# Memory attention and an erf-softplus FFN: blocks of 384 tokens across batches, and the second product with g stationary

## The chip, the cores and the metric

The kernel runs on one core of a Trainium2 chip. The metric is the device time of one execution in microseconds (us). Engines are named as in the profile: PE multiplies matrices (PEld is its loading of the stationary operand), ACT applies functions to tiles, DVE does arithmetic on tiles, POOL is hardly used, SP issues the DMAs in order.

## What is computed

Eight batches of 576 tokens, 8 heads of 64 dimensions, 32 memory slots a head. The attention gathers k and v into the slots with a softmax over the tokens, and reads them with a softmax over the slots; the FFN (512 to 2048 to 512) follows on all 4608 tokens.

```python
a = softmax(phi, axis=tokens)                  # (b, h, s, m)
k_m = einsum('bhsm,bhsd->bhmd', a, k); v_m = einsum('bhsm,bhsd->bhmd', a, v)
attn = softmax(q @ k_m.T / 8, axis=slots)
x = (attn @ v_m), heads side by side           # (4608, 512)
h = x @ w_in
g = h * erf(softplus(h))
out = g @ w_out                                # (4608, 512)
```

The weights come as 64-bit floats; the kernel reads them as pairs of 32-bit words.

## The kernel before

**Operands.** Products that must be exact enough are made from two parts: `split` (L114 to L116) puts a rounded copy in `hi` (ACT, type fp32r) and the rest in `lo` (DVE), and `products` (L374) takes hi x hi, hi x lo and lo x hi. So each product below is three matmuls. `erf(softplus(h))` is a product of a tanh and three factors (`FACTORS`, L29): `ffn1` makes the tanh (L397, ACT) and the first product (L398, DVE), `factor` the three others (L411 or L413 on ACT, L414 on DVE), `g_split` the two parts of g (L422 ACT, L423 DVE).

**Folding.** `vw` (L317) multiplies v_m of a batch with w_in once, so that the first FFN product runs over the 256 slots (8 heads x 32) of the attention weights instead of over 512 dimensions. `heads` (L302) does it for 8 heads, four at a time in one of two row halves; the scores (L335) use it too. One `vw_pair` makes 512 of the 2048 hidden columns; a batch has four pairs. The pool `vwp` holds four pairs.

**Steps.** The unit `u` is half a batch, U = 288 tokens, so there are 16 units, and each is taken in NPR = 8 chunks of 256 hidden columns: NS = 128 steps. Step `i` issues `ffn1(i, 0)`, a factor of step i-1, `ffn1(i, 1)`, two more factors, `g_split(i-2)`, and merged with these `ffn2(i-3, d)` for the four blocks d of 128 output columns. `ffn1` is 12 matmuls of 128x128 stationary (vw) by 128x288 moving (attention weights). `ffn2` is 24 matmuls with w_out stationary and g (128x288) moving; it adds up in four PSUM tiles over the eight chunks of a unit, which are then copied out (L453) and stored transposed (L454, `outT`).

**Side work.** The attention of a later unit or batch lies in lists by step (`batch_tasks` L456, `unit_tasks` L467) and is merged into the steps before it is needed: `phi_max`, `phi_exp` (the softmax over tokens), `kmvm`, `block_diag` (k_m and v_m in the layout of `heads`), `vw_pair`, and for each unit `scores`, `sm_max`, `sm_norm`, `sm_back`. In the first eight steps the weights are decoded too: `decode_1` (DVE L142, ACT L145 and L146), `decode_2` (DVE L159 and L162), `decode_3` (w_out only: ACT L174, PE L177 and L178, ACT L179). The weights come in 20 pieces, 12 of 1 MB and 8 of 512 KB; LEAD = 7 of them are decoded ahead of step 0.

**Order.** The list `prog` is the order in which the work is written. The tile framework then orders each engine's queue with a time model of its own, taking ready work forward; for DVE a window (`WINDOW`) limits by how much. SP's queue is in the order that results. Loads are written as soon as a buffer of their kind has room (`fill`, `frees`, `loads`); `FIRST` is the order of the first ones.

**Memory.** Tiles come from pools with a fixed number of buffers; a tile that takes a buffer waits for the last reader of the tile that had it. `f` (three buffers) holds a factor; `ost` (two buffers) holds outputs until they are stored; `gp` (three buffers) holds g.

Of the kernel before, what the change touches and what calls it, by code (L numbers as in the profile page):

```python
# [25 lines left out]


# [9 lines left out]
def tile_memory_attention_then_erf_softplus_ffn(  # L37
# [3 lines left out]
    k: bass.AP,  # L41
    v: bass.AP,
# [4 lines left out]
    outT: bass.AP,  # L47
# [4 lines left out]
    H = k.shape[2]  # L52
# [3 lines left out]
    DM = outT.shape[0]  # L56
    NDM = DM // P
    NP_ = H // 2
    NG = 2
    U = S // 2  # L60
    NB = U // 32
    NPR = DFF // 256
    NU = 2 * B
    NS = NU * NPR
    NF = len(FACTORS)
    SC = [(c * P, min(P, S - c * P)) for c in range((S + P - 1) // P)]
    RAW_BUFS = 3
    STAGED = 6
    FIRST = "wo phiT start phi wo raw raw wo raw start wo q".split()
    LEAD = 7  # L70
    WINDOW = {mybir.EngineType.DVE: (12, 28)}
    PO = 5
    SO = 2
    VL = 4
    VB = 1
# [4 lines left out]
    vwp = ctx.enter_context(tc.tile_pool(name="vwp", bufs=NPR // 2))  # L80
# [4 lines left out]
    gp = ctx.enter_context(tc.tile_pool(name="gp", bufs=3))  # L85
    raw_pool = ctx.enter_context(tc.tile_pool(name="raw", bufs=RAW_BUFS))
    ost = ctx.enter_context(tc.tile_pool(name="ost", bufs=2))
    ps_h = ctx.enter_context(tc.tile_pool(name="ps_h", bufs=2, space=PSUM))
    ps_o = ctx.enter_context(tc.tile_pool(name="ps_o", bufs=1, space=PSUM))
    ps_a = ctx.enter_context(tc.tile_pool(name="ps_a", bufs=2, space=PSUM))  # L90
# [8 lines left out]
    def column(value, name):  # L99
        t = const.tile([P, 1], F32, name=name)  # L100
        nc.vector.memset(t, value)
        return t

    tb = column(GB, "tb")
    fb = [column(f[1] if f[0] == "Q" else f[2], f"fb{i}") for i, f in enumerate(FACTORS)]
# [14 lines left out]
    def load_weight(*key):  # L120
        name, c, r, n = key
        if n == NP_:
            t = wop.tile([P, NP_ * 256], I64, name="w_" + name, tag="wo")
        else:
            t = raw_pool.tile([P, n * 256], I64, name="raw")
        if name == "in":
            nc.sync.dma_start(
                out=t.rearrange("p (r f) -> p r f", r=n),
                in_=w_in[:, r : r + n, c * 256 : (c + 1) * 256],
            )  # L130
        else:
            nc.sync.dma_start(
                out=t.rearrange("p (r d) -> p r d", d=DM),
                in_=w_out[:, 2 * c + r : 2 * c + r + n // 2],
            )
        st[key] = t

    def decode_1(*key):
        v = st[key].bitcast(I32).rearrange("p (n two) -> p n two", two=2)
        lo, hi = v[:, :, 0], v[:, :, 1]  # L140
        hf = hi.bitcast(F32)
        nc.vector.tensor_scalar(  # L142
            out=hf, in0=hf, scalar1=TOP, scalar2=-TOP, op0=ALU.min, op1=ALU.max
        )
        nc.scalar.activation(lo, lo.bitcast(U32), AF.Identity, scale=LOW)  # L145
        nc.scalar.activation(hf, hf, AF.Identity, scale=REBIAS)  # L146

    def decode_2(*key):
        name, c, r, n = key
        v = st[key].bitcast(I32).rearrange("p (n two) -> p n two", two=2)  # L150
        lo, hi = v[:, :, 0], v[:, :, 1]
        dst = hi
        if name == "in":
            if r == 0:
                if c % 2 == 0:
                    w_in_sb[c // 2] = const.tile([P, NP_, 512], F32, name=f"w_in{c // 2}")
            dst = w_in_sb[c // 2].bitcast(I32)[:, r : r + n, c % 2 * 256 : (c % 2 + 1) * 256]
            hi, lo = (x.rearrange("p (r f) -> p r f", f=256) for x in (hi, lo))
        nc.vector.scalar_tensor_tensor(  # L159
# [4 lines left out]
        )  # L164

    def decode_3(*key):
        name, c, r, n = key
        t = st.pop(key)
        if name == "out":
            w = t.bitcast(F32).rearrange("p (r d two) -> p r d two", d=DM, two=2)[:, :, :, 1]  # L170
            if r == 0:
                wo[c] = wop.tile([P, 2, 2, DM], F32R, name="wo", tag="wo")
            hi, lo = (wo[c][:, x, r : r + n // 2] for x in range(2))
            nc.scalar.activation(hi, w, AF.Identity)  # L174
            for x in range(n // 2):
                ps = ps_a.tile([P, DM], F32, name="psa")
                nc.tensor.matmul(out=ps, lhsT=ident, rhs=w[:, x], start=True, stop=False)  # L177
                nc.tensor.matmul(out=ps, lhsT=minus, rhs=hi[:, x], start=False, stop=True)  # L178
                nc.scalar.activation(lo[:, x], ps, AF.Identity)  # L179

    def load_phiT(b, g):
        if (b, g) == (0, 1):
            t = wop.tile([P, S], F32, name="phiT", tag="wo")
        else:
            t = att.tile([P, S], F32, name="phiT")
# [3 lines left out]
    def load_phi(b):  # L189
        t = att.tile([P, len(SC), H * M], F32, name="phi")  # L190
        n = S // P
        s0, ln = SC[-1]
        nc.sync.dma_start(
            out=t[:, :n], in_=phi[b, : n * P].rearrange("(c p) e -> p c e", p=P)
        )
        if ln < P:
            nc.sync.dma_start(out=t[:ln, n], in_=phi[b, s0 : s0 + ln])
        st["a", b] = t

    def load_kv(b, p):  # L200
        if b == 0 and p == NP_ - 1:
            t = wop.tile([P, len(SC), 2, 2, D], F32, name="kv", tag="wo")
        else:
            t = raw_pool.tile([P, len(SC), 2, 2, D], F32, name="raw")
        n = S // P
        s0, ln = SC[-1]
        h = 2 * p
        for x, src in enumerate((k, v)):
            src = src[b, :, h : h + 2]
            nc.sync.dma_start(  # L210
                out=t[:, :n, x], in_=src[: n * P].rearrange("(c p) h e -> p c h e", p=P)
            )
            if ln < P:
                nc.sync.dma_start(out=t[:ln, n, x], in_=src[s0 : s0 + ln])
        for j in range(2):
            st["kv", b, h + j] = t[:, :, :, j, :]

    def load_q(u):
        b, hf = divmod(u, 2)
        t = att.tile([P, NP_, U], F32, name="q")  # L220
        nc.sync.dma_start(
            out=t, in_=qT[b, :, hf * U : (hf + 1) * U].rearrange("(p r) s -> r p s", r=P)
        )
        st["q", u] = t
# [77 lines left out]
    def heads(w, x, n):  # L302

        ps = [ps_a.tile([P, n], F32, name="psa") for _ in range(2)]
        for p in range(NP_):
            for par in range(2):
                rows = slice(par * D, (par + 1) * D)
                nc.tensor.matmul(  # L308
                    out=ps[par][p * M : (p + 1) * M, :],
# [5 lines left out]
        return ps  # L315

    def vw(b, c, n=1):  # L317
        if c % 2 == 0:
            st["vw2", b, c // 2] = [
                vwp.tile([P, 2, 512], F32R, name=f"vw_{x}") for x in ("hi", "lo")  # L320
            ]
        hi, lo = st["vw2", b, c // 2]
        cols = slice(c % 2 * 256, (c % 2 + n) * 256)
        for par, ps in enumerate(heads(vm[b % 2], w_in_sb[c // 2][:, :, cols], n * 256)):
            split(hi[:, par, cols], lo[:, par, cols], ps)
        for x in range(c, c + n):
            f = slice(x % 2 * 256, (x % 2 + 1) * 256)
            st["vw", b, x] = (hi[:, :, f], lo[:, :, f])
# [6 lines left out]
    def scores(u):  # L335
        s = st["s", u] = att.tile([P, NG, U], F32, name="sc")
        for g, ps in enumerate(heads(km[u // 2 % 2], st.pop(("q", u)), U)):
            nc.vector.transpose(out=s[:, g, :], in_=ps)
# [24 lines left out]
    def sm_back(u):  # L363
        s = st.pop(("s", u))
        hi = atp.tile([P, NG, U], F32R, name="at_hi")
        lo = atp.tile([P, NG, U], F32R, name="at_lo")
        t = el.tile([P, NG, U], F32, name="f", bufs=3)
# [9 lines left out]
    def ffn1(i, j):  # L377
        u, c = divmod(i, NPR)
        at, w = st["at", u], st["vw", u // 2, c]
        if j == 0:  # L380
            st["el", i] = (
                el.tile([P, 2, U], F32, name="tt"),
# [261 lines left out]
```

## Time and profile before

| | |
|---|---|
| median of 3 runs | 791.84 us (790.88 to 793.14) |
| the profiled execution | 790.4 us, of which the span is 788.5 us |
| granted TensorE clock, mean | 0.985 |
| instructions | 15764, of them 6192 matmuls |
| moved by DMA | 64.99 MB, mean 82 GB/s |

The span is the time between the first and the last instruction of the profiled execution. Busy times are sums over an engine's instructions without their overlap; the chain is the line of work that ended last, followed back to what released each piece. The names are those of the program's tiles: `psh` and `pso` are the PSUM tiles of the first and the second FFN product, `psa` those of all the rest, `wo` is w_out decoded and split, `at` the attention weights, `raw` a staging buffer for k, v and weights. The form "128*128 128x288" of a matmul is its stationary and its moving operand.

### The profile page before, as it was taken

What the parts mean: (1) busy time and instruction counts of PE and PEld (TensorE: products, weight loads), DVE (VectorE), ACT (ScalarE), POOL (GpSimd) and SP (SyncE); (2) the same over time, 40 slices, a digit from 0 to 9 for tenths busy, and PEclk for the clock granted to TensorE, in tenths of its full rate; (3) what the DMA queues carried; (4) which work ended last, traced back from release to release, by engine and by line L of the source; (5) the groups of instructions that cost most, each with busy time, mean ns of one, the idle gap of its engine ahead of it and who ended that gap; (6) DMA issues with size and microseconds to landing.
All of it is one profiled execution on the core that took longest, in us unless ns stands there. A gap on an engine that the chain in (4) does not pass through costs nothing.

```text
span 788.5 us, 15764 instructions
## 1 busy us (share of the span) xinstructions
PE 750.3 (95%) x6192; PEld 666.4 (85%) x6192; DVE 663.6 (84%) x1145; ACT 632.7 (80%) x1164; POOL 0.7 (0%) x6
## 2 busy tenths in 40 slices
PE   2668899999999999999999999999999999999998
PEld 1246678789988899888988899889988899889998
DVE  4699787889979897988979798989979897889874
ACT  4699778678887878878887878878888888788784
POOL 0000000000000000000000000000000000000000
PEclk9986999999999999999999999999999999999999
DMA  9983326303060203302060203302060201100000
GB/s 275 359 316 107 86 87 171 100 1 91 13 200 1 75 18 106 106 1 91 19 193 2 76 17 109 104 1 91 18 194 1 77 1 54 40 1 31 2 31 31
DMA packets 69514, 64.99 MB, mean 82 GB/s; under 512 B 4160, under 2 KB 62016, under 8 KB 68672
## 3 DMA queue, kind: packets, MB, share of 16 engines
q1 hardware_dynamic: 69440, 63.98, 26.2%
q8 instruction: 49, 0.80, 0.4%
q14 instruction: 25, 0.20, 0.1%
HBM read 54.53 MB, written 9.44 MB: 81 GB/s over the span
## 4 chain that ended last, share of the span: by engine, by line
PE 85%; ACT 7%; DMA 5%; DVE 2%; SPq 1%; issue 1%; ACTq 0%; DVEq 0%
PE pso L437 49%; PE psh L390 25%; PE psa L308 6%; PE psa L275 3%; DMA phiT<-phiT 1%; DMA w_in<-w_in 1%; DMA raw<-k 1%; PE psa L177 1%; DMA raw<-v 1%; DVE acc L414 1%; ACT f L413 1%; ACT tt L397 1%; ACT wo L179 1%; ACT w_in L145 1%; ACT w_out L146 1%
## 5 line engine op out<-in xcount | busy, mean ns | idle before, releaser
L437 PE MATMUL pso<-g_hi,wo 128*128 128x288 f32 x2048 | 436.3, 298 | 1.0 <-ACT g_hi L422 1.0
L437 PEld LDWEIGHTS pso<-g_hi,wo 128*128 128x128 f32 x2048 | 336.7, 189 | 26.5 <-issue 13.6
L414 DVE SCALAR_TENSOR_TENSOR acc<-f,acc 128x576 f32<-128x576 f32 x384 | 289.7, 754 | 34.7 <-ACT f L411 10.6
L437 PE MATMUL pso<-g_lo,wo 128*128 128x288 f32 x1024 | 302.3, 296 | 1.0 <-DVE g_lo L423 1.0
L437 PEld LDWEIGHTS pso<-g_lo,wo 128*128 128x128 f32 x1024 | 193.7, 189 | 2.6 <-DVE g_lo L423 1.3
L413 ACT ACTIVATE f<-tt,fb 128x576 f32<-128x576 f32 x256 | 185.1, 766 | 1.9 <-DVE acc L414 1.9
L397 ACT ACTIVATE tt<-psh,tb 128x288 f32<-128x288 f32 x256 | 121.9, 497 | 44.3 <-PE psh L390 43.0
L398 DVE SCALAR_TENSOR_TENSOR acc<-tt,psh 128x288 f32<-128x288 f32 x256 | 111.1, 449 | 23.6 <-ACT tt L397 22.9
L423 DVE SCALAR_TENSOR_TENSOR g_lo<-acc,g_hi 128x576 fp32r<-128x576 f32 x128 | 96.2, 751 | 28.7 <-ACT g_hi L422 25.9
L390 PE MATMUL psh<-at_hi,vw_hi 128*128 128x288 f32 x512 | 116.2, 308 | 4.3 <-ACT at_hi L115 2.6
L422 ACT ACTIVATE g_hi<-acc 128x576 fp32r<-128x576 f32 x128 | 87.3, 682 | 39.8 <-DVE acc L414 33.7
L390 PE MATMUL psh<-at_lo,vw_hi 128*128 128x288 f32 x512 | 110.9, 298 | 0.0
L390 PE MATMUL psh<-at_hi,vw_lo 128*128 128x288 f32 x512 | 109.8, 296 | 0.0
L390 PEld LDWEIGHTS psh<-at_hi,vw_hi 128*128 128x128 f32 x512 | 82.5, 191 | 23.3 <-DVE acc L414 10.1
L411 ACT ACTIVATE f<-tt,fb 128x576 f32<-128x576 f32 x128 | 99.5, 778 | 3.1
L390 PEld LDWEIGHTS psh<-at_hi,vw_lo 128*128 128x128 f32 x512 | 83.4, 190 | 2.8 <-issue 2.4
L390 PEld LDWEIGHTS psh<-at_lo,vw_hi 128*128 128x128 f32 x512 | 83.3, 191 | 0.9 <-issue 0.8
L308 PE MATMUL psa<-w_in,vm 64*32 64x512 f32 (+1 forms) x576 | 42.6, 561 | 6.1 <-ACT wo L179 4.7
L116 DVE TENSOR_TENSOR vw_lo<-psa,vw_hi 128x512 fp32r<-128x512 f32 (+1 forms) x72 | 43.0, 624 | 1.1 <-ACT vw_hi L115 0.9
L115 ACT ACTIVATE vw_hi<-psa 128x512 fp32r<-128x512 f32 (+1 forms) x72 | 36.2, 547 | 5.8 <-PE psa L308 5.7
L453 ACT ACTIVATE ot<-pso 128x288 f32<-128x288 f32 x60 | 23.2, 402 | 12.2 <-DMA outT<-ot 11.8
L275 PE MATMUL psa<-raw,phi 128*32 128x128 f32 x620 | 28.8, 291 | 3.5 <-ACT phi L259 2.4
(73 smaller groups left out, 437.6 us busy)
## 6 DMA issues: line engine op xcount, KB each, us to landing
q<-qT SPq DMA_DIRECT2D x16, 576.0 KB, 4.2
outT<-ot SPq DMA_DIRECT2D x60, 144.0 KB, 2.5
raw<-k SPq DMA_DIRECT2D x31, 256.0 KB, 3.4
raw<-v SPq DMA_DIRECT2D x31, 256.0 KB, 3.7
w_in<-w_in SPq DMA_DIRECT2D x6, 1024.0 KB, 8.7
w_out<-w_out SPq DMA_DIRECT2D x6, 1024.0 KB, 10.2
phiT<-phiT SPq DMA_DIRECT2D x16, 288.0 KB, 4.2
phi<-phi SPq DMA_DIRECT2D x8, 512.0 KB, 5.3
```

The lines of the kernel that those rows point to most:

```text
L116: nc.vector.tensor_tensor(out=lo, in0=src, in1=hi.bitcast(F32), op=ALU.subtract)
L275: nc.tensor.matmul(out=ps[M * j : M * (j + 1), 0, :], lhsT=a[:ln, c, (4 * g + j) * M : (4 * g + j + 1) * M], rhs=kvt[j][:ln, c], start=(c ...
L308: nc.tensor.matmul(out=ps[par][p * M : (p + 1) * M, :], lhsT=w[rows, p, :], rhs=x[rows, p, :], start=True, stop=True,)
L390: nc.tensor.matmul(out=ps, lhsT=x[:, g, j * P : (j + 1) * P], rhs=y[:, g, :], start=(k + g == 0), stop=(k == len(parts) - 1 and g == NG - 1),)
L397: nc.scalar.activation(tt[:, j], ps, AF.Tanh, bias=tb, scale=0.5)
L398: nc.vector.scalar_tensor_tensor(out=acc[:, j], in0=tt[:, j], scalar=1.0, in1=ps, op0=ALU.add, op1=ALU.mult)
L411: nc.scalar.activation(f, tt, AF.Square, bias=fb[n])
L413: nc.scalar.activation(f, tt, AF.Tanh, bias=fb[n], scale=FACTORS[n][1])
L414: nc.vector.scalar_tensor_tensor(out=acc, in0=f, scalar=fd[n], in1=acc, op0=ALU.add, op1=ALU.mult)
L422: nc.scalar.activation(hi, acc, AF.Identity, scale=GC)
L423: nc.vector.scalar_tensor_tensor(out=lo, in0=acc, scalar=GC, in1=hi.bitcast(F32), op0=ALU.mult, op1=ALU.subtract)
L437: nc.tensor.matmul(out=o, lhsT=x[:, d * P : (d + 1) * P], rhs=y[:, j, :], start=(c + j + k == 0), stop=(c == NPR - 1 and j == 1 and k == l ...
```

## The change

The unit becomes a block of W = 384 consecutive tokens of all 4608: 12 blocks, 96 steps. A block can lie across two batches (blocks 1, 4, 7 and 10, with 192 tokens of each; `SPANS` lists the parts). In such a block `scores` and the first product are taken in parts, each with its own batch's k_m or vw.

In the second product g becomes the stationary operand, 128 tokens at a time, and 512 columns of w_out move, so the output has tokens on its partitions and is stored as it is, in three tiles of 128 tokens a block. It is copied out into a buffer of `f`. The biases of the tanh and the factors are numbers instead of columns in memory.

k and v are stacked on the host, two heads of k and v side by side, and tokens are given to partitions in runs of four, for phi as well, so that a partition's rows lie together. The weights come in 16 pieces of 1 MB, w_in in the pool of vw, and LEAD is 4. `vwp` has 5 buffers (of 2 parts each), `raw` 4, which also take phi and phiT, `gp` 2, `ps_a` 3 instead of 2. The steps at which the attention is done move with the blocks.

```diff
-    U = S // 2
-    NU = 2 * B
-    NS = NU * NPR
+    W = 384
+    ND = W // P
+    NW = B * S // W
+    NS = NW * NPR
...
-    RAW_BUFS = 3
-    STAGED = 6
-    FIRST = "wo phiT start phi wo raw raw wo raw start wo q".split()
-    LEAD = 7
+    RAW_BUFS = 4
+    VW_BUFS = 5
+    FIRST = "vw raw wo raw raw raw wo wo q wo vw wo vw wo".split()
+    LEAD = 4
...
-    fb = [column(f[1] if f[0] == "Q" else f[2], f"fb{i}") for i, f in enumerate(FACTORS)]
+    fb = [f[1] if f[0] == "Q" else f[2] for f in FACTORS]
...
+    def load_tokens(t, src):
+        n = S // P
+        ln = SC[-1][1]
+        nc.sync.dma_start(
+            out=t[:, :n], in_=src[: n * P].rearrange("(p c) e -> p c e", c=n)
+        )
+        if ln < P:
+            nc.sync.dma_start(out=t[:ln, n], in_=src[n * P :])
...
-        ps = ps_h.tile([P, U], F32, name="psh")
-        parts = products(w, at)
-        for k, (x, y) in enumerate(parts):
-            for g in range(NG):
-                nc.tensor.matmul(
-                    out=ps,
-                    lhsT=x[:, g, j * P : (j + 1) * P],
-                    rhs=y[:, g, :],
...
+        ps = ps_h.tile([P, W], F32, name="psh")
+        o = 0
+        for b, s0, n in SPANS[w]:
+            parts = products(st["vw", b, c], at)
+            for k, (x, y) in enumerate(parts):
+                for g in range(NG):
+                    nc.tensor.matmul(
+                        out=ps[:, o : o + n],
+                        lhsT=x[:, g, j * P : (j + 1) * P],
+                        rhs=y[:, g, o : o + n],
...
-        nc.scalar.activation(tt[:, j], ps, AF.Tanh, bias=tb, scale=0.5)
+        nc.scalar.activation(tt[:, j], ps, AF.Tanh, bias=GB, scale=0.5)
...
-            parts = products([wo[c][:, x, j] for x in range(2)], g)
+            parts = products(g, [x[:, j] for x in wo[c]])
             for k, (x, y) in enumerate(parts):
                 nc.tensor.matmul(
                     out=o,
-                    lhsT=x[:, d * P : (d + 1) * P],
-                    rhs=y[:, j, :],
+                    lhsT=x[:, j, d * P : (d + 1) * P],
+                    rhs=y,
...
-                t = ost.tile([P, U], F32, name="ot")
-            nc.scalar.activation(t, st.pop(("o", u, d)), AF.Identity)
-            nc.sync.dma_start(out=outT[d * P : (d + 1) * P, u * U : (u + 1) * U], in_=t)
+            t = el.tile([P, DM], F32, name="f", bufs=3)
+            nc.scalar.activation(t, st.pop(("o", w, d)), AF.Identity)
+            r = w * W + d * P
+            nc.sync.dma_start(out=out[r : r + P], in_=t)
...
+    for w in range(1, NW):
+        late = 2 if w == 1 else 0
+        for n, f in enumerate((scores, sm_max, sm_norm, sm_back)):
+            at_step(min((w - 1) * NPR + 3 + late + n, w * NPR - 1), f, w)
...
+        for c in range(0, NPR, 2):
+            early = 1 if SPANS[w][0][0] != b and c else 3
+            at_step(w * NPR + c - early, vw_pair, b, c)
...
-    prog = [(phi_max, 0, 0), (phi_max, 0, 1), (phi_exp, 0)]
+    prog = d[:1] + [(phi_max, 0, 0), (phi_max, 0, 1)] + [(phi_exp, 0)]
+    d.remove((decode_2, "in", 0))
+    prog += [(decode_2, "in", 0)]
     for g in range(NG):
-        prog += [(kmvm, 0, g)] + d[g : g + 1] + [(block_diag, 0, g)]
-    prog += merge([x for ts in unit_tasks(0) for x in ts], d[2:])
-    prog += [(vw, 0, c) for c in range(VB)]
+        prog += [(kmvm, 0, g), (block_diag, 0, g)]
+    prog += [(scores, 0), (vw, 0, 0), (sm_max, 0)] + d[1:4]
+    prog += [(sm_norm, 0)] + d[4:6] + [(sm_back, 0)] + d[6:]
```

In the step at which a pair of vw is made for a split block, `early = 1` puts it one step ahead of its own first use.

321 lines of the change are left out of this document (150 added, 171 removed).

## The prediction, made before the change was run

> **What bounds the kernel now.** I read the page's busy shares and its chain first, then the busy times by stage, then the chain and the timeline inside the stages.
>
> ```profile
> span 788.5 us, 15764 instructions
> PE 750.3 (95%) x6192; PEld 666.4 (85%) x6192; DVE 663.6 (84%) x1145; ACT 632.7 (80%) x1164; POOL 0.7 (0%) x6
> PE 85%; ACT 7%; DMA 5%; DVE 2%; SPq 1%; issue 1%; ACTq 0%; DVEq 0%
> PE pso L437 49%; PE psh L390 25%; PE psa L308 6%; PE psa L275 3%; DMA phiT<-phiT 1%; DMA w_in<-w_in 1%; DMA raw<-k 1%; PE psa L177 1%; DMA raw<-v 1%; DVE acc L414 1%; ACT f L413 1%; ACT tt L397 1%; ACT wo L179 1%; ACT w_in L145 1%; ACT w_out L146 1%
> ```
>
> PE carries 85% of the chain, nearly all of it in the two products (L437, L390). ACT and DVE are at 80% and 84%, but only 9% of the chain is theirs. Where that 9% lies is seen in the busy times by stage (columns: stretch, its length, PE, PEld, DVE, ACT and POOL busy with their counts, granted clock, DMA share, GB/s):
>
> ```profile
> 0.00:20.00 20.00, 4.52 (x44) 2.88 (x44) 9.74 (x21) 9.57 (x14) 0.70 (x6) 1.00 0.91 276
> 20.00:40.00 20.00, 13.00 (x74) 5.51 (x71) 12.82 (x17) 13.80 (x25) 0.00 (x0) 1.00 1.01 361
> 40.00:60.00 20.00, 13.94 (x85) 7.85 (x83) 18.98 (x28) 19.97 (x31) 0.00 (x0) 0.80 0.79 300
> 60.00:80.00 20.00, 16.72 (x78) 13.23 (x79) 20.00 (x33) 18.68 (x29) 0.00 (x0) 0.69 0.33 106
> 80.00:100.00 20.00, 17.79 (x125) 12.54 (x124) 16.05 (x32) 15.09 (x31) 0.00 (x0) 0.91 0.33 97
> 100.00:120.00 20.00, 20.00 (x145) 15.88 (x144) 16.02 (x35) 15.44 (x32) 0.00 (x0) 1.00 0.32 90
> 405.00:493.00 88.00, 87.38 (x756) 80.39 (x757) 75.79 (x134) 71.33 (x136) 0.00 (x0) 1.00 0.23 66
> ```
>
> There are two stages. From about 120 us on PE never rests (87.4 of 88 us for one batch), so nothing that ACT, DVE or DMA save there counts. Before 120 us PE waits: first for loads, then for ACT and DVE, which turn the weights from 64-bit numbers into floats (decode) beside the first eight steps. The timeline gives these marks: the first product of step 0, the first of step 8, and the last eviction.
>
> ```profile
> 45.98 0.85 PE L390 MATMUL psh<-at_hi,vw_hi 128*128 128x288 f32 x2 [2.60 <-ACT at_hi L115]
> ...
> 123.03 0.42 PE L390 MATMUL psh<-at_hi,vw_hi 128*128 128x288 f32 x2
> ...
> 785.25 0.41 ACT L453 ACTIVATE f<-pso 128x288 f32<-128x288 f32 x1 [0.19 <-PE pso L437]
> ```
>
> The chain inside the first stage (start, time, what):
>
> ```profile
> 16.54 7.48 DMA raw<-v
> ...
> 24.04 9.54 DMA w_in<-w_in
> ...
> 33.60 1.18 ACT w_in L145
> ...
> 39.16 0.95 ACT wo L179 x2
> 40.12 1.06 ACT w_out L146
> ...
> 50.85 0.78 ACT tt L397 x2
> ...
> 51.66 0.78 ACT f L411
> 52.43 1.33 ACT f L413 x2
> ...
> 56.33 1.07 ACT wo L174
> ...
> 57.88 0.57 ACT g_hi L422
> ...
> 118.17 0.90 PE psa L177 x2
> 119.07 0.23 PE psa L178
> ...
> 120.01 3.18 PE pso L437 x24
> ```
>
> From 33.6 us on the chain is ACT, instruction behind instruction. These are the true costs of one on ACT: 1.06 us for a decode pass of 1024, 0.48 for an eviction, 0.39 for a tanh of 288, 0.67 for a factor, 0.57 for g_hi.
>
> **The change on PE.** The number of moving columns stays: 3072 x 288 = 1728 x 512 in the second product, 1536 x 288 = 768 x 384 + 768 x 192 in the first. (12 blocks of 8 steps; 4 blocks lie across two batches and take every first product in two halves of 192.) So the widths decide. 24 products of 288 take 3.18 us: 132 ns. One of 512 in the same reduced type (L178) takes 230 ns. A line through both has 0.4375 ns a column and 6 ns fixed; it gives 174 ns for 384 and 90 ns for 192. But a weight load stands before each product:
>
> ```profile
> 394.38 0.27 PEld L291 LDWEIGHTS psa<-ident,kvk 128*128 128x128 f32 x2
> 394.62 0.19 PEld L437 LDWEIGHTS pso<-g_hi,wo 128*128 128x128 f32 x1
> 394.73 0.19 PEld L437 LDWEIGHTS pso<-g_lo,wo 128*128 128x128 f32 x1
> ```
>
> Behind a product of only 128 columns the next load starts 110 ns after the one before (394.62 to 394.73): the load, not the columns, sets the pace there. I take 110 ns for 192 columns; bounds are 90 (columns alone) and 132 (no cheaper than 288).
> - second product: 1728 x 230 = 397.4 us for 3072 x 132 = 405.5: -8.1
> - first product, 384 wide: 768 x 174 = 133.6 for 1024 x 132 = 135.2: -1.6
> - first product, 192 wide: 768 x 110 = 84.5 for 512 x 132 = 67.6: +16.9
>
> Together +7.2 us: on PE the change loses. The split blocks have the same number of first products as before, each two thirds as wide, below what hides a weight load.
>
> The Trainium skill (TensorE: Matmul & The Clock Gate, Back-to-back issue gap) puts a warm product at columns / 2.4 + 2.5 ns. It would give 122.5 ns for 288 and 215.8 for 512, where the trace has 132 and 230; by the Trainium skill the second product would cost 1728 x 14 = 24 us less than in my sum.
>
> **The change on ACT and DVE.** A step now holds 384 tokens, so there are 96 steps for 128.
>
> ```profile
> L397 ACT ACTIVATE tt<-psh,tb 128x288 f32<-128x288 f32 x256 | 121.9, 497 | 44.3 <-PE psh L390 43.0
> L453 ACT ACTIVATE ot<-pso 128x288 f32<-128x288 f32 x60 | 23.2, 402 | 12.2 <-DMA outT<-ot 11.8
> L413 ACT ACTIVATE f<-tt,fb 128x576 f32<-128x576 f32 x256 | 185.1, 766 | 1.9 <-DVE acc L414 1.9
> L350 ACT ACTIVATE sc<-sc 128x576 f32<-128x576 f32 x16 | 10.8, 673 | 0.9 <-DVE sc L347 0.9
> L115 ACT ACTIVATE vw_hi<-psa 128x512 fp32r<-128x512 f32 x56 | 30.2, 588 | 5.8 <-PE psa L308 5.7
> L116 DVE TENSOR_TENSOR vw_lo<-psa,vw_hi 128x512 fp32r<-128x512 f32 x56 | 36.6, 684 | 0.9 <-ACT vw_hi L115 0.9
> ```
>
> At one shape an ACT instruction with a bias column takes 93 to 95 ns more (497 to 402, 766 to 673). L350 has a bias that is a number (0), so I take a number as bias to cost nothing: 5 instructions a step, 0.47 us a step. If the number still comes from memory, nothing is saved. Width costs 0.83 ns a column ((588 - 402) / 224). ACT's chain costs for a full step become tanh 2 x 0.38, factors 3 x 0.73, g_hi 0.73 = 3.7 us, against 0.78 + 2.0 + 0.57 = 3.35 now, for a third more tokens. After 120 us this is off the path. Before it is the bound.
>
> **The first stage.** *Loads.* Before the last k and v arrive (24.0), the queue now carries three weight pieces, phiT, phi, k and v: 6.7 MB. The change puts one weight piece before them: 4.6 MB, at 276 GB/s some 17 us, and k and v come in runs of 4 KB instead of 512 bytes, with half the issues. The scores can start some 6 us earlier. Their softmax is a third longer (+2 us) and has fewer decode passes between its parts on DVE (2 weights fewer). I put the first product at 37 us for 46 (bounds 33 and 46).
>
> *Steps 0 to 7.* ACT from step 0 to step 8 now: FFN 8 x 1.45 + 7 x 1.33 + 6 x 0.57 = 24; decode of what is left (8 large and 8 half pieces) 35; vw 4; next batch 5; sum 68 of the 77 us that pass, so 9 us are waits. After: FFN 8 x 1.49 + 7 x 1.46 + 6 x 0.73 = 26.5; decode (two thirds of the second pair, then six pairs at 2.1 + 4.1) 39; vw 4; batch 1, now needed at step 8, 8.5; sum 78. With waits between 0 and 11 us step 8 starts between 115 and 126; I take 121. Between 80 and 120 us ACT is now busy only 30.5 of 40 us; wider steps fill that.
>
> **The sum.** From step 8 on PE bounds, as now. Main products: 32 split steps x 24 x 0.110 = 84.5; 56 x 12 x 0.174 = 116.9; the second product of steps 5 to 95, 91 x 18 x 0.230 = 376.7; together 578.1. (Before: 120 x 12 + 123 x 24 = 4392 x 0.132 = 579.7; the rest of PE's work until 785.2 is 82.5 for seven batches.) Of these 82.5 some 5 now lie before step 8: 77.5. I add 3 for vw in split blocks (below) and 4.5 for the end (3.3 now; one eviction of 512, 256 KB to land). 121 + 578.1 + 77.5 + 3 + 4.5 = 784.1 against 788.5. With the 1.9 us that lie around the span (790.4) that is 786.0; the median of the runs is 1.4 above the profiled one, so 787.
>
> *Costed at nothing:* the six PE evictions fewer (off PE); the heads of the scores (16 groups, same columns); the output, which now takes one of three f buffers and holds it until its DMA lands: ACT's next factor waits behind it some 2 us, as ot does now (11.8 us in the L453 row) without PE stopping; PE has the second product of older steps to do. If that cover is gone it is 12 blocks x 2 = 24 us. g has 2 buffers instead of 3: g_split of a step comes behind the tanh of the same step, which comes behind the products that read the old buffer.
>
> **Rivals.**
> - *Just-in-time vw.* There are 5 vw buffers. In a split block a new pair can be written only when the old batch has used up a pair, one step before its own first use: two evictions and a subtraction, 0.59 + 0.59 + 0.68 = 1.9 us. If the heads are ordered behind the last second product of the step and nothing fills, PE stops 4 blocks x 3 pairs x 1.9 = 23 us: 804. For it: the program lists them there. Against: the second product of the next step is ready, and the build order does move ready work forward. I keep 3 us. Slower.
> - *The start is not shorter.* ACT's sum to step 8 grows (78 for 68), and an earlier first product only brings ACT's queue forward. With step 8 at 128: 791. It decides from 124.4 on.
> - *Narrow products.* At 132 ns for 192 columns: +17, 801.
> - *Cheaper wide products.* L177, full 32 bit, takes 0.45 us a record; if a record is two passes over 512 columns, a pass takes 0.225, and 384 columns 0.169: -12, 772. The Trainium skill's rule stands on this side too (760 by its 215.8 ns); that 288 takes 132 and not its 122.5 speaks against it.
> - *A shorter start.* Step 8 at 112, no waits and the first product at 34: 775.
>
> **How the numbers follow.** About 0.3% (2.4 us) is what a measurement here tells from no change: 789.5 to 794.2. In medians, 3.3 above the spans: forecast (783 to 791) 0.36; start not shorter (794, half of it same, half slower) 0.22; just-in-time (807) 0.15; narrow (804) 0.07; cheaper wide products (775) 0.12; shorter start (778) 0.08. Faster 0.36 x 0.85 + 0.12 + 0.08 = 0.50; same 0.05 + 0.11, rounded to 0.17; slower 0.11 + 0.15 + 0.07 = 0.33. The range 773 to 804 leaves out the just-in-time case at its full price (0.15); narrow products and cheaper wide ones lie at its ends.
>
> **What would show it.** Right: in the chain, runs of second products at 0.23 us each; in split blocks first products at 0.11; the first product near 37 and step 8 near 121; tanh near 480 ns at 384 columns, factors near 835 at 768; PE busy all the time behind that. Wrong: PE idle behind ACT vw_hi or DVE vw_lo in split blocks; ACT waiting on the output's DMA with PE behind it; 192 columns at 132 or more; step 8 later than 124.

## The result, and the profile after

The changed kernel takes 822.71 us (median of 4 runs, 822.1 to 824.04) where the kernel before took 792.49 us in the same sitting (790.88 to 793.7): a ratio of 1.0385 (95% interval 1.036 to 1.041). It is slower by about 30 us. The prediction said 787.0 with a range of 773 to 804; the result lies outside the range, on the other side of no change.

The page of the changed kernel, its busy shares and its chain:

```profile
span 822.2 us, 12335 instructions
PE 779.2 (95%) x4848; PEld 597.0 (73%) x4848; DVE 641.8 (78%) x897; ACT 555.6 (68%) x926; POOL 0.7 (0%) x6
PE 86%; DMA 7%; DVE 3%; ACT 2%; issue 1%; SPq 1%; DVEq 0%; ACTq 0%
```

The trace has 1344 matmuls fewer, and PE is busy 28.9 us longer (779.2 for 750.3). ACT is busy 77 us less, and that buys nothing. So the question is which matmuls take longer. The busy time by stage (columns as in the prediction's table):

```profile
0.00:20.00 20.00, 3.74 (x44) 2.59 (x44) 6.65 (x14) 7.46 (x12) 0.70 (x6) 1.00 0.87 286
20.00:40.00 20.00, 13.30 (x98) 5.45 (x95) 11.82 (x16) 15.74 (x28) 0.00 (x0) 0.74 1.02 404
40.00:60.00 20.00, 13.29 (x64) 9.13 (x65) 18.20 (x32) 16.60 (x27) 0.00 (x0) 0.66 1.05 365
60.00:80.00 20.00, 14.02 (x89) 7.67 (x88) 20.00 (x24) 20.00 (x31) 0.00 (x0) 0.74 0.31 95
...
120.00:140.00 20.00, 20.00 (x117) 11.64 (x115) 12.73 (x19) 10.55 (x17) 0.00 (x0) 1.00 0.14 40
140.00:160.00 20.00, 17.10 (x79) 10.84 (x78) 12.90 (x18) 10.18 (x16) 0.00 (x0) 0.68 0.23 71
...
460.00:560.00 100.00, 100.00 (x647) 78.70 (x639) 79.66 (x114) 66.99 (x115) 0.00 (x0) 1.00 0.18 59
```

The two stages are still there. Behind the start PE never rests, and ACT has a third of its time free; that much is as predicted. The start is longer. The chain of the steady stage shows what PE does with its time:

```profile
407.14 2.11 PE psh L395 x12
409.25 4.12 PE pso L443 x18
413.37 0.78 PE psa L306 x8
...
427.29 0.97 PE psa L306 x2
428.26 2.04 PE pso L443 x8
430.30 0.97 PE psa L306 x2
431.28 2.31 PE psh L395 x12
433.58 1.01 PE psa L306 x12
...
443.78 1.01 PE psa L306 x14
...
448.94 0.97 PE psa L306 x2
```

The two large products run as predicted: 18 second products in 4.12 us are 229 ns each, 12 first products of 384 in 2.11 us are 176 ns each. The lines to look at are those of L306, the heads. `heads` writes eight matmuls for a group, and a whole group stands in the trace as 16 records: each of these full 32-bit matmuls leaves two. So `x2` is one heads matmul and `x14` seven. One of them costs 0.97 us, and seven cost 1.01 us. In the kernel before most groups of 512 columns run whole, and another matmul comes only behind the 16 records:

```profile
274.44 1.09 PE L308 MATMUL psa<-w_in,vm 64*32 64x512 f32 x16
275.46 0.40 PE L437 MATMUL pso<-g_hi,wo 128*128 128x288 f32 x1
```

After the change a single matmul of such a group stands between second products, twice within 3 us (timeline of PE):

```profile
427.22 1.04 PE L306 MATMUL psa<-w_in,vm 64*32 64x512 f32 x2
428.19 0.50 PE L443 MATMUL pso<-wo,g_lo 128*128 128x512 f32 x1
...
430.23 1.04 PE L306 MATMUL psa<-w_in,vm 64*32 64x512 f32 x2
```

A heads matmul uses a corner of the array (64 rows, 32 columns). Eight of them on different corners run at the same time, so a group takes hardly longer than one of them; call that time a pass (here about 1 us). When the build order pulls one of the eight out and puts it elsewhere, that one takes a whole pass by itself. Below, a group is called torn when that happens, and a run is a stretch of heads matmuls with no other matmul between them. The Trainium skill (TensorE: Matmul & The Clock Gate, Measured speedup vs the span model) says that a pack of tiles on different positions takes one matmul's duration plus some 4 ns a tile. The trace agrees in kind: seven matmuls take 1.01 us and one takes 0.97, so six tiles more cost 40 ns, some 7 ns each. It also shows that the same rule makes a lone tile as dear as a pack.

In the order that the build gave PE, the heads stand in 66 runs before and in 82 after; with no group torn they would be 52 and 48, so the kernel before has torn groups too. Taking the time from each matmul's start to the next one's start, and adding it up by kind over the whole trace:

| us | before | after | difference |
|---|---|---|---|
| first product | 213.9 | 239.6 | +25.7 |
| second product | 423.3 | 414.3 | -9.0 |
| heads | 67.2 | 80.6 | +13.4 |

(All else is within some 3 us. Waits of PE are counted to the matmul ahead of them.) Of the 25.7 us of the first product, 10.5 lie ahead of step 8 (28.5 for 18.0): there a step is a third wider and PE waits. Of the 13.4 us of the heads, 12.1 are those of vw (61.2 for 49.1) and 1.3 those of the scores (19.4 for 18.1).

### The profile page after: what moved, and what is told of

Same layout as the page of the kernel before. It is cut to its first block, busy times and chain, and to the rows that moved or that the text cites. A ratio compares the mean times of both kernels' runs of the same rounds, so it can differ in the third digit from the quotient of the medians.

```text
span 822.2 us, 12335 instructions
## 1 busy us (share of the span) xinstructions
PE 779.2 (95%) x4848; PEld 597.0 (73%) x4848; DVE 641.8 (78%) x897; ACT 555.6 (68%) x926; POOL 0.7 (0%) x6
## 4 chain that ended last, share of the span: by engine, by line
PE 86%; DMA 7%; DVE 3%; ACT 2%; issue 1%; SPq 1%; DVEq 0%; ACTq 0%
PE pso L443 48%; PE psh L395 27%; PE psa L306 8%; DMA phiT<-phiT 3%; PE psa L273 2%; DMA kv<-kv 2%; DMA w_in<-w_in 2%; DVE acc L420 1%; PE psa L177 1%; DVE w_out L158 0%; DVE w_out L161 0%; PE psa L240 0%; SPq L132 0%; DVE acc L406 0%; PE psa L289 0%
## 5 line engine op out<-in xcount | busy, mean ns | idle before, releaser
L443 PE MATMUL pso<-wo,g_hi 128*128 128x512 f32 x1152 | 363.8, 401 | 4.9 <-ACT g_hi L428 4.9
L420 DVE SCALAR_TENSOR_TENSOR acc<-f,acc 128x768 f32<-128x768 f32 x288 | 274.3, 953 | 44.7 <-ACT f L417 16.9
L443 PEld LDWEIGHTS pso<-wo,g_hi 128*128 128x128 f32 x1152 | 213.2, 190 | 72.3 <-issue 19.2
L395 PE MATMUL psh<-at_hi,vw 128*128 128x192 f32 (+1 forms) x1024 | 216.8, 313 | 4.3 <-ACT at_hi L117 3.1
L443 PE MATMUL pso<-wo,g_lo 128*128 128x512 f32 x576 | 219.4, 396 | 0.0
L395 PEld LDWEIGHTS psh<-at_hi,vw 128*128 128x128 f32 x1024 | 167.9, 193 | 32.5 <-issue 8.2
L419 ACT ACTIVATE f<-tt 128x768 f32<-128x768 f32 x192 | 153.4, 834 | 1.6 <-DVE acc L420 1.6
L406 DVE SCALAR_TENSOR_TENSOR acc<-tt,psh 128x384 f32<-128x384 f32 x192 | 103.4, 550 | 62.8 <-ACT tt L405 62.5
L443 PEld LDWEIGHTS pso<-wo,g_lo 128*128 128x128 f32 x576 | 108.4, 189 | 29.6 <-DVE psm L261 2.5
L395 PE MATMUL psh<-at_lo,vw 128*128 128x192 f32 (+1 forms) x512 | 117.1, 310 | 1.0 <-DVE at_lo L118 1.0
L428 ACT ACTIVATE g_hi<-acc 128x768 fp32r<-128x768 f32 x96 | 80.6, 840 | 53.5 <-DVE acc L420 32.1
L429 DVE SCALAR_TENSOR_TENSOR g_lo<-acc,g_hi 128x768 fp32r<-128x768 f32 x96 | 91.4, 952 | 22.8 <-ACT g_hi L428 21.6
L417 ACT ACTIVATE f<-tt 128x768 f32<-128x768 f32 x96 | 81.2, 846 | 4.7 <-DMA out<-f 1.4
L306 PE MATMUL psa<-w_in,vm 64*32 64x512 f32 (+1 forms) x576 | 59.6, 572 | 1.9 <-DVE w_in L161 1.9
L454 ACT ACTIVATE f<-pso 128x512 f32<-128x512 f32 x36 | 21.3, 593 | 10.7 <-PE pso L443 10.5
L177 PE MATMUL psa<-w_out,ident 128*128 128x512 f32 x32 | 22.5, 803 | 4.6 <-issue 4.5
```

The lines of the kernel that those rows point to most:

```text
L306: nc.tensor.matmul(out=ps[par][p * M : (p + 1) * M, o : o + n], lhsT=w[rows, p, :], rhs=x[rows, p, :], start=True, stop=True,)
L395: nc.tensor.matmul(out=ps[:, o : o + n], lhsT=x[:, g, j * P : (j + 1) * P], rhs=y[:, g, o : o + n], start=(k + g == 0), stop=(k == len(par ...
L406: nc.vector.scalar_tensor_tensor(out=acc[:, j], in0=tt[:, j], scalar=1.0, in1=ps, op0=ALU.add, op1=ALU.mult)
L417: nc.scalar.activation(f, tt, AF.Square, bias=fb[n])
L419: nc.scalar.activation(f, tt, AF.Tanh, bias=fb[n], scale=FACTORS[n][1])
L420: nc.vector.scalar_tensor_tensor(out=acc, in0=f, scalar=fd[n], in1=acc, op0=ALU.add, op1=ALU.mult)
```

## The experiments

Each was timed beside the kernel before on the same chip; "ratio" is to that kernel, with its 95% interval.

**First round: is it vw that comes late, the narrow products, the turned second product, or the rest?** In the first two kernels below a split block takes its first products from the old batch's vw alone, so that nothing waits for the new one.

`wide_free`: also in one part of 384 columns instead of two of 192.

```diff
-        for b, s0, n in SPANS[w]:
+        old = SPANS[w][0][0]
+        for b, s0, n in [(old, 0, W)]:
             parts = products(st["vw", b, c], at)
```

> The kernel after, but in the four blocks that lie across two batches the first product takes the old batch's vw for all 384 tokens (this replaces part of the computation): 12 products of 384 columns a step for 24 of 192, and no first use of the new batch's vw in that block. Theory A (the split blocks cost: narrow products and a deadline on vw): the trace after has 0.111 us for 192 and 0.174 for 384 columns, 32 steps x (24 x 0.111 - 12 x 0.174) = 18 us, and the heads of vw take 12.0 us for two batches where before had 8.2, 3.8 x 4 = 15 us; so 822.7 - 18 - (12 to 15) = 790 to 793. Theory B (the split costs only its columns, the rest is lost elsewhere): 822.7 - 18 = 805.

Measured 800.7 us, ratio 1.0122 (1.0099 to 1.0145): between the two.

`narrow_free`: two parts of 192, as in the changed kernel.

```diff
-            parts = products(st["vw", b, c], at)
+            parts = products(st["vw", SPANS[w][0][0], c], at)
```

> The kernel after, but both halves of a split block take the old batch's vw (this replaces part of the computation): still 24 products of 192 columns, but nothing in the block waits for the new batch's vw. Theory A (deadline on vw costs): 822.7 - (12 to 15) = 808 to 811. Theory B (no deadline cost, the longer heads come from something else): 820 to 823.

Measured 820.3 us, 1.0366 (1.0349 to 1.0383). Together: without the deadline on vw at most 2.4 us go (1.5 by the ratios, and their intervals overlap), and with the narrow products gone too another 19.6. The theory that vw comes late falls. The narrow products cost about what the prediction's sum has for them (17.7 us: 84.5 for 192 wide against 66.8 for half as many of 384), and that sum came out faster. So something else costs some 30 us.

`wout_stat`: the second product turned back, w_out stationary and 384 columns of g moving, with four output tiles and so two PSUM buffers for the rest.

```diff
-    ps_a = ctx.enter_context(tc.tile_pool(name="ps_a", bufs=3, space=PSUM))
+    ps_a = ctx.enter_context(tc.tile_pool(name="ps_a", bufs=2, space=PSUM))
...
-            parts = products(g, [x[:, j] for x in wo[c]])
+            parts = products([x[:, j] for x in wo[c]], g)
...
-                    lhsT=x[:, j, d * P : (d + 1) * P],
-                    rhs=y,
+                    lhsT=x[:, d * P : (d + 1) * P],
+                    rhs=y[:, j, :],
```

> The kernel after with the second product turned back: w_out stationary, 384 columns of g moving, four tiles of 128 output columns, stored transposed (PSUM for the attention back to 2 banks, which the fourth tile needs). By the trace's rates 24 x 0.174 = 4.18 us a step for 18 x 0.230 = 4.14. Theory A (the turn is neutral): 820 to 828. Rival C (512 columns moving cost on every change to another product, 318 ns for 224, and the stores in f buffers hold ACT): 812 or less.

Measured 815.32 us, 1.0301 (1.0279 to 1.0323): between the two. Its heads stand in 69 runs, not 82, and this is what led to the theory of torn groups.

`loads_bias`: the kernel before with only the loads in long runs and the numbers as biases.

```diff
-    k: bass.AP,
-    v: bass.AP,
+    kv: bass.AP,
...
-        nc.scalar.activation(tt[:, j], ps, AF.Tanh, bias=tb, scale=0.5)
+        nc.scalar.activation(tt[:, j], ps, AF.Tanh, bias=GB, scale=0.5)
```

> The kernel before with two parts of the change alone: k and v stacked and loaded in long runs, and the biases as numbers. Theory A (after 120 us only PE counts; before it the attention chain and the decode on DVE set the pace): 788 to 792, at most 3 us gained. Rival D (ACT sets the pace of the first eight steps, 0.47 us a step saved, and the loads come 6 us earlier): 780 to 786.

Measured 795.2 us, 1.0051 (1.0036 to 1.0067). Both expectations missed: two edits that add no work made the kernel slower. Heads: 73 runs for 66.

**Second round: torn groups.** `whole_after`: the changed kernel with ordering constraints on PE that keep each group of heads together and let no other PE work move across it. `near` is a constraint on the order alone, without a semaphore.

```diff
+        mine = [x for x in traced[start:] if x.engine == mybir.EngineType.PE]
+        if f in (vw, vw_pair, scores):
+            for x in since:
+                tc.add_manual_dep(mine[0], x.name, near, reason="whole group")
+            for x, y in zip(mine, mine[1:]):
+                tc.add_manual_dep(y, x.name, near, reason="whole group")
+            last, since = mine[-1], []
+        else:
+            for x in mine:
+                if last is not None:
+                    tc.add_manual_dep(x, last.name, near, reason="whole group")
+                since.append(x)
```

> The kernel after, with ordering constraints on PE alone: the matmuls of one heads group (8 tiles of 64x32 that run at the same time) follow one another with no other matmul between them, and no PE work is moved across a group. Theory E (torn groups): the build order of the kernel after puts the groups in 82 runs where 48 would do, and in the trace a run of 2 matmuls takes the same 0.97 us as one of 16; 34 runs less give 20 to 28 us on the heads. Against it stands that the group now comes strictly before the first product that needs it, 1.9 us in 12 places, up to 23 us. So 798 to 820, with the heads' time in the trace at 43 to 55 us for 80.6. Rival F (the runs are long because PE would wait there anyway): 820 or more, the time moves to other rows.

Measured 799.37 us, 1.0101 (1.0069 to 1.0133): within Theory E's range. The heads took 60.7 us, above its 43 to 55. Start to start, the heads fell by 20 us and the first products by 13; the small matmuls of the attention and the decode rose by 11, all ahead of step 8, where the heads now wait 10 us for the decode (`ACT wo L179` in the last of the four rows below).

`torn_after`: the other direction. The heads get a higher priority one matmul at a time, so that the build order pulls single ones forward.

```diff
-                nc.tensor.matmul(
+                with tc.high_priority(offset=60):
+                    nc.tensor.matmul(
```

> The kernel after, with a higher priority for the heads in the build's ordering, which tears them more: 111 runs for 82. Theory E: 29 more runs at 0.9 us each: 845 to 850. Rival F (the pieces fill time in which PE would wait): 818 to 828.

Measured 848.24 us, 1.0727 (1.07 to 1.0754). That is within Theory E's range. The same 576 records of vw's heads, in the groups of the pages of four kernels (before, after, torn, whole):

```profile
L308 PE MATMUL psa<-w_in,vm 64*32 64x512 f32 (+1 forms) x576 | 42.6, 561 | 6.1 <-ACT wo L179 4.7
```
```profile
L306 PE MATMUL psa<-w_in,vm 64*32 64x512 f32 (+1 forms) x576 | 59.6, 572 | 1.9 <-DVE w_in L161 1.9
```
```profile
L307 PE MATMUL psa<-w_in,vm 64*32 64x512 f32 (+1 forms) x576 | 87.1, 581 | 2.7 <-DVE w_in L161 2.7
```
```profile
L306 PE MATMUL psa<-w_in,vm 64*32 64x512 f32 (+1 forms) x576 | 41.0, 572 | 10.8 <-ACT wo L179 10.0
```

The mean of one record hardly differs (561 to 581 ns); how many of them overlap does. The order alone takes the busy time of this row from 41.0 to 87.1 us. Added up from start to start, with the scores' forms, the heads take 60.7, 80.6 and 105.8 us in 48, 82 and 111 runs (whole, after, torn); the medians are 799.4, 822.7 and 848.2. A run more costs 0.6 to 0.9 us of heads, and the whole time 0.7 to 0.9. That torn groups cost this is shown in both directions. In the steady stage (block 4 to block 7, two batches) it is 176.3, 182.7 and 193.7 us (whole, after, torn), where the kernel before takes 176 to 177.

`whole_loads_bias`: the same constraints on `loads_bias`.

> The kernel before with the loads in long runs and the biases as numbers (795.2 as it stood, with 73 runs of heads where before has 66), and the groups kept whole: 52 runs. Theory E: the 7 runs more were its 4 us; with 21 runs less 795 - 15 = 780, if nothing else waits. Rival F: 793 to 797.

Measured 803.79 us, 1.0169 (1.0134 to 1.0204). Missed: the heads fell to 61.8 us as they should, but the second product rose from 420.1 to 434.0. In this kernel the constraint has a price of its own; `loads_scores_whole` below looks for it.

`loads_alone`: the kernel before with the loads of k, v and phi in long runs alone (one line of the edit).

```diff
-            out=t[:, :n], in_=phi[b, : n * P].rearrange("(c p) e -> p c e", p=P)
+            out=t[:, :n], in_=src[: n * P].rearrange("(p c) e -> p c e", c=n)
```

> The kernel before with the loads in long runs alone: 65 runs of heads, as before (66). Theory E: 788 to 791, since nothing is torn and the start is set by the attention chain and the decode. Rival G (the loads themselves cost something, for example issues or a later weight): 794 to 796.

Measured 789.46 us (10 runs), 0.9979 (0.9966 to 0.9991); heads in 65 runs: Theory E. The loads in long runs bring 1.6 us. This is the only kernel here with the whole computation that is faster than the kernel before, and so faster than both.

**Third round: the rest, with the groups kept whole.** `whole_wide`: `whole_after` with the edit of `wide_free`.

> Whole groups (as in the run of that name) and, in the split blocks, the old batch's vw for all 384 tokens (this replaces part of the computation): 12 products of 384 for 24 of 192. If narrow products and torn groups are two separate costs, 799.4 - 32 x (24 x 0.111 - 12 x 0.174) = 781, and the steady two batches take 171 to 172 us for 176. Rival: with whole groups the deadline on vw is part of it too, 770 or less.

Measured 777.79 us, 0.9829 (0.9809 to 0.9849): 21.6 us less than `whole_after`, 3 more than expected; two steady batches take 170.9 us for 176.3, and the rival falls. This is the price of the narrow products and of the deadline on vw together, with no groups torn; the prediction's terms make it 17.7 and 3.

`whole_wout`: `whole_after` with the edit of `wout_stat`.

> Whole groups, and the second product turned back (w_out stationary, four tiles, two PSUM banks for the attention instead of three). Theory E: the 7 us that the turn back gave before were its fewer torn runs (69 for 82); with none torn the turn is worth nothing by columns (24 x 0.174 = 4.18 for 18 x 0.230 = 4.14 us a step), and with two banks the groups wait: 800 to 810. Rival C (the turned product costs by itself): 790 to 794.

Measured 807.65 us, 1.0213 (1.0193 to 1.0233): with whole groups, turning the second product back loses 8.3 us, as Theory E expected. So the turn is not what made the changed kernel slow. The widths explain 3.5 us of it (2304 products of 384 at 0.174 are 400.9 us, 1728 of 512 at 0.230 are 397.4); the rest may come from the PSUM buffer that is given up with it, which was not tried by itself.

`whole_start`: `whole_after`, but block 1 is computed from batch 0 alone, so that batch 1 is due eight steps later (its attention is written six steps later).

```diff
+    SPANS[1] = [(0, 384, 384)]
...
+    FIRST_W[1] = 2
```

> Whole groups, and block 1 computed as if it belonged to batch 0 alone (this replaces part of the computation): batch 1's attention and vw are due eight steps later, at block 2. Narrow products of one block go: 8 x (24 x 0.111 - 12 x 0.174) = 4.6 us. Theory H (the longer start comes from batch 1 being due at step 8, within the stage that ACT and DVE set): step 8 at 140 or earlier for 150.7, in all 787 or less. Rival I (it comes from w_in, which has two staging buffers): step 8 near 148, in all 794 to 796.

Measured 791.57 us (10 runs), 1.0015 (1.0002 to 1.0029): 7.8 us less than `whole_after`. Of these 4.6 are block 1's narrow products (192 x 0.111 = 21.3 us became 96 x 0.174 = 16.7). Its step 8 begins at 136.93 us on the timeline, for 150.68 in `whole_after`. Step 8 comes as Theory H has it, but much of batch 1's work has only moved behind it; the time lies between the two expectations. With batch 1 due later, 3.2 us (7.8 - 4.6) of the longer start go, not all. The two theories are not kept apart either: in this run the last w_in also lands earlier, at 85.8 us for 103.3, and between the first product and step 8 ACT waits 0.6 us for w_in, for 7.9.

`bias_alone`: the kernel before with only numbers as biases (the second half of `loads_bias`' diff).

> The kernel before with the biases as numbers alone: ACT's tanh 402 and factor 673 ns for 497 and 766. The build order has 71 runs of heads for 66. Theory E: 5 runs more cost 4 to 5 us, the biases gain at most 2: 792 to 796. Rival: ACT sets the first eight steps, 786 to 789.

Measured 796.68 us, 1.0064 (1.0042 to 1.0086). Each tanh and factor is some 90 ns shorter on an engine that is off the path, and the kernel is slower by 5 to 6 us, just above Theory E's range: the build order came out with 71 runs of heads for 66, and the heads took 73.6 us for 67.2. The heads' 6.4 us are as much as the loss, so the price looks like that of the order, not of the edit; keeping the groups whole in this kernel was not tried.

**Fourth round: two open points.** `whole_pool`: `whole_after` with the loads of w_in issued from POOL's queue, to see whether they are late because they stand behind other loads in SP's.

```diff
-            nc.sync.dma_start(
+            nc.gpsimd.dma_start(
```

> Whole groups, with the loads of w_in issued from POOL's queue instead of SP's, where in the whole-groups run two phiT loads of batch 1 held the queue for 17.8 us (73.1 to 90.9) and the last w_in left at 94.5. Theory I (w_in behind waiting loads): the last w_in is decoded by 90 for 103, step 8 starts at 140 to 145 for 150.7, in all 790 to 795. Rival H (batch 1's work and the decode on ACT and DVE set the pace): 797 to 801.

Measured 812.34 us, 1.0279 (1.0246 to 1.0311). Both missed, for another reason (timeline of POOL):

```profile
13.80 0.75 POOL L125 DMA_DIRECT2D w_in<-w_in  x1 [11.63 <-issue]
26.24 0.75 POOL L125 DMA_DIRECT2D w_in<-w_in  x1 [11.69 <-issue]
27.08 0.31 POOL masks.py:199 TENSOR_SCALAR_AFFINE_SELECT ident<-ident 128x128 f32<-128x128 f32 x1
```

POOL stands idle over 11 us ahead of each of these loads, waiting for nothing that the profile shows, and the making of `ident` stands behind them. ACT's waits:

```profile
ACT minus L102 <- POOL ident masks.py:199: 20.6, 1, 20.6
```

So the first product moves from 47.6 to 64.8. The last w_in lands later than it did (109.1 for 103.3), so the run does not do what it was meant to. From the first product to step 8 it takes 96.8 us for 103.1. The run does not tell the two theories apart.

`loads_scores_whole`: `loads_alone` with only the groups of the scores kept together.

```diff
-        if f in (vw, vw_pair, scores):
+        if f is scores:
```

> The kernel before with the loads in long runs, and only the heads groups of the scores kept whole (54 runs for 65; the vw groups are free, as they were hardly torn). Theory E: the scores' heads fall from 3.8 to 2.6 us in two batches, 11 runs less: 789.5 - (4 to 8) = 782 to 786. Rival (the constraint makes PE wait for PSUM banks, as with all groups kept whole in two banks, 803.8): 792 or more.

Measured 812.99 us, 1.0266 (1.0246 to 1.0286). The rival's range. The groups are whole (40.9 us in the row of the heads), but now PE stops (its waits, and one stretch of the steady stage):

```profile
PE pso L430 <- ACT ot L446: 16.9, 11, 3.0
```
```profile
350.00:450.00 100.00, 97.35 (x824) 89.56 (x823) 85.15 (x148) 79.86 (x148) 0.00 (x0) 0.98 0.19 60
```

No PE work may cross a group, so nothing fills the wait for an output's eviction: 16.9 of the 23.5 us that are lost against `loads_alone`, where PE's longest waits do not have this row. In this kernel, keeping the groups whole in this way costs more than it saves.

## Why the prediction was wrong

**The steps that failed.** The profiled span is 822.2 us where the sum has 784.1, 38.1 more. Two terms of the sum make it up:
- The start: "step 8 ... I take 121". It begins at 146.2, 25.2 us later.
- "The rest of PE's work until 785.2 is 82.5 for seven batches", carried over as 77.5. From step 8 to the end 676.0 us pass where the sum has 663.1, 12.9 more. The heads alone take 57.1 us there, and took 44.8 behind step 8 before.

Against the forecast the start is the larger miss. Against the kernel before the torn groups are, because the sum counted on a gain at the start: step 8 2 us earlier than before, with 96 tokens more done.

**The heads.** The prediction carries the term over without a word on vw's heads; its reason for the heads of the scores, "same columns", holds for both. But the price of a group is one pass for each run into which the build order breaks it, and a new program gets a new order: 66 runs became 82, +13.4 us of heads. Nearly all of it is vw's heads, in the 77.5; the heads of the scores, which the prediction lists as "costed at nothing", are 1.3 us dearer. Keeping the groups whole is worth more than these 13.4, namely 23.3 us (822.7 - 799.4): the heads then take 60.7 us, less than the 67.2 in the kernel before, which has torn groups itself. From step 8 to the end `whole_after` takes 647.4 us, less than the 663.1 of the sum. No rival had this mechanism. The prediction names the reordering ("the build order does move ready work forward"), but only as something that fills waits, and gives it no cost.

**The start.** "I put the first product at 37 us": it is at 52.2. "Step 8 ... I take 121": it starts at 146.2, and at 150.7 in `whole_after`. The loads did come earlier (the last k and v land at 19.6 us, where it was 25.7; the prediction's 24.0 is an earlier v), but the scores as a whole could not use that. Chain and timeline of the changed kernel's start:

```profile
1.47 8.88 DMA phiT<-phiT
10.37 7.47 DMA kv<-kv
...
47.75 1.07 ACT w_out L144
48.81 0.75 ACT phiT L230 x2
...
51.31 0.84 ACT at_hi L117
52.19 2.94 PE psh L395 x8
```
```profile
30.23 1.19 PE L306 MATMUL psa<-q,km 64*32 64x384 f32 x4 [2.71 <-ACT km L293]
...
49.90 0.49 PE L240 MATMUL psa<-diag,ones 128*128 128x128 f32 x2 [1.44 <-ACT diag L234]
...
146.21 0.69 PE L395 MATMUL psh<-at_hi,vw 128*128 128x192 f32 x4 [1.95 <-ACT at_hi L117]
```

The second half of the scores waits for km (30.2, when all of them began before), which ACT makes in the order that the build gave it, behind decode. From there to the first product it takes 22 us, because decode of w_out and the softmax of batch 1 (phiT L230) stand between the parts of block 0's softmax on ACT and DVE. My step moved one end of a queue and took the rest as rigid. That is 15.2 of the 25.2 us. The other 10.0 lie between the first product and step 8, in this stretch (before, then after; columns as in the prediction's table):

```profile
45.98:123.03 77.05, 69.19 (x432) 52.03 (x433) 67.94 (x122) 66.20 (x115) 0.00 (x0) 0.85 0.41 131
52.19:146.21 94.02, 85.24 (x497) 55.22 (x497) 76.02 (x103) 68.69 (x113) 0.00 (x0) 0.91 0.32 105
```

The prediction had 78 us of ACT's work here and "waits between 0 and 11 us". ACT works 68.7 us, less than that, and stands idle 25.3, of which 8.3 us are waits for the DMA of w_in and 7.9 for PE's first product. Some of the work was done ahead of the later first product (and the decode term comes to 41 by its own prices, not 39); what failed is the waits. The granted clock was not lower than before in this stretch (0.91 for 0.85). The rival "the start is not shorter" named this and put step 8 at 128; that was too little by 18 us. Between 120 and 160 us PE also loses to torn groups and to block 1's softmax (17.1 of 20 us busy in 140 to 160, at a granted clock of 0.68). `whole_after` is 8.4 us slower than the kernel before, and two batches of its steady stage take 176.3 us, as before (176 to 177): so that rest lies in the start. Part of it may be the constraint's own price there, since its step 8 begins 4.5 us later than the changed kernel's. `whole_start` takes 3.2 of the 8.4 us off. What the rest is stays open: w_in that lands late, which the chain of the changed kernel suggests, or the work of ACT and DVE on the way.

```profile
76.93 5.68 DMA w_in<-w_in
82.64 1.16 ACT w_in L144
...
90.90 8.85 DMA w_in<-w_in
99.77 1.20 ACT w_in L144
```

**What was right.** The rates of PE: median 230, 174 and 111 ns for 512, 384 and 192 columns, as worked out (230, 174, 110); the rival with 132 ns and that of cheaper wide products are out. In two steady batches the first products take 3.8 us more than before and the second 2.3 less; a quarter of the sum's 15.3 and -8.1 is 3.8 and -2.0. That the weight load sets the pace of the narrow products is the prediction's reading of the loads' 110 ns; no run here changes the load alone. The Trainium skill (TensorE: Matmul & The Clock Gate, LDWEIGHTS) has columns / 1.2, 107 ns for 128, and the trace is 4 ns above it. ACT's instructions, too:

```profile
L405 ACT ACTIVATE tt<-psh 128x384 f32<-128x384 f32 x192 | 93.2, 490 | 135.0 <-PE psh L395 133.4
L419 ACT ACTIVATE f<-tt 128x768 f32<-128x768 f32 x192 | 153.4, 834 | 1.6 <-DVE acc L420 1.6
```

490 ns for about 480, 834 for 835; a number as bias costs nothing that shows. Just-in-time vw was rightly held at 3 us (at most 2.4 measured, for its 23). The outputs through `f` do not stop PE (ACT waits once for such a store, 1.4 us). That PE bounds the steady stage was right as well: with whole groups, two batches take what they took before. There the first products cost 3.4 us more than before, and the second product and the heads give 2.7 and 1.3 back.

**The ledger**, by the ratios to the kernel before (791 us), since the kernels were timed in different sittings: the changed kernel is 30.5 us slower, of which 22.5 go with whole groups and 8.0 stay, mostly in the longer start. By the medians it is 31.7, 23.3 and 8.4. Of the gains, that of the loads is 1.6 us, measured in the kernel before; ACT's shows nowhere, since it is off the path.

## What to carry to other kernels

Where small matmuls run side by side on corners of the array, their price here was a pass for each unbroken run (one matmul 0.97 us, seven 1.01), not for each column: after any edit, count these runs in the order that the build gives, before trusting a sum of columns. An edit that only shortens work off the path came with a loss of 5 us here and with another order, so a part that "can only help" needs a run of its own. A first transfer that lands earlier is worth what the next engine's queue lets through; follow the queue's written order up to the instruction that sets the end.

## What the hardware showed beside this

- One heads matmul between others takes 0.97 us and seven take 1.01. From the start of a product of 512 columns to that of heads behind it 318 ns pass, behind one of 288 columns 224. That is some 90 ns more than to the next product of the same width (230 and 132): the change from full products to corner tiles costs about the same behind both.
- Loads of 1 MB issued from POOL's queue came over 11 us behind each other (13.80, 26.24), and other work of POOL waits behind them.
- Between 20 and 40 us the granted clock was 0.74 in the changed kernel and 1.00 before, at nearly the same busy time of PE (13.30 and 13.00 us). In `whole_after` it was 1.00 there too, with 13.75 us. Each is one profiled execution, and no run was made to find out why.
- Ordering constraints without any semaphore cost 23.5 us in one kernel (`loads_scores_whole`, 812.99 for 789.46) and are worth 22 to 23 in another (`whole_after`): what they forbid can matter as much as what they order.
